# A prologue in a new order, one more softmax half summed on ScalarE, and slots 6 to 11 of a fused attention and MoE kernel rearranged

## The chip, the core and the metric

The kernel runs on one core of a Trainium2 chip. The metric is the device time of one execution in microseconds (us). TensorE (PE) multiplies, VectorE (DVE), ScalarE (ACT) and GpSimd (POOL) do the elementwise work, and SyncE (SP) issues most of the transfers from and to HBM. Each engine works through its own queue in the order in which the program issued its instructions; engines wait for each other by semaphores.

## The reference

Three stages, each fed by the one before it, in float32:

```python
# 1. chunked attention: q, k, v are (8 batches, 8 heads, 576, 64), in chunks of 64 rows
scores = scale * q_c @ k_c.T                      # 64x64 for each chunk
attn = exp(scores - max(scores)); attn /= sum(attn) + 1e-9
x = attn @ v_c                                    # -> (8, 576, 512)
# 2. gated feed-forward with a convolution over 3 neighbouring rows
h = relu(x @ w_in)                                # (8, 576, 1024)
gate = sigmoid(conv3(h))                          # each of the 1024 columns by itself
x = (h * gate) @ w_out                            # (8, 576, 512)
# 3. spatial gating
h = relu(x @ w_in2); u, v = h[..., :512], h[..., 512:]
v_s = w_spatial @ layernorm(v) + b_spatial
out = (u * v_s) @ w_out2
```

The four weight matrices come as float64 words, which the kernel turns into float32 itself.

## The kernel before

The 4608 rows of stages 1 and 2 are cut into ten tiles (eight of 512 rows, two of 256). Stage 2 of a tile has eight column blocks of 128, and **a slot is one tile and one column block**: slot s is tile s // 8 and block s % 8. Slots 0 to 7 are the first tile, 8 to 15 the second. A second phase (stage 3) follows, which the change does not touch.

To multiply float32 at the fast rate, each operand is split in a high and a low part (`xh`, `xl`; `w1h`, `w1l`; `gh`, `gl`; `w2h`, `w2l`), and a product is three terms: high by high, and the two mixed ones. The high part is a ScalarE cast, the low part a subtraction on VectorE (L83, `split_lo`) or, for some weights, on GpSimd. In a slot stand:

- **in(s)**, `moe_in`, L465: x times the block of w_in into the PSUM tile `h`, twelve matmuls of 512 columns. There are two such PSUM buffers.
- **h**, `moe_h`, L491: ScalarE's relu (`hh`, L498) and the middle tap of the convolution (`c`, L502), then two taps on VectorE (L517). From slot 8 on two edge elements at batch borders are mended on ScalarE (`m`, L513, and the "fix", L526).
- **g**, `moe_tanh` and `moe_g`, L523 and L530, for the slot before: ScalarE's tanh, VectorE's product (L532).
- **split**, `moe_split`, L535: `gh` on ScalarE, `gl` on VectorE.
- **out(s)**, `moe_out`, L552: the gated block times w_out, added up over a tile's eight blocks in four PSUM banks `acc`. The first five slots use plain float32 (`w2f`), all others three terms, twelve matmuls of 512 columns. After a tile's last block four ScalarE copies (`x`, L573) empty the banks.

The attention of one tile is two groups of 256 rows (group g; 0 and 1 belong to the first tile, 2 and 3 to the second, 4 and 5 to the third). The steps of a group are spread over the slots ahead of the tile that needs it. They are: scores `s` (L262); for each half j of the heads the softmax, which is the maximum and the subtraction on VectorE (L277, L283), the exp on ScalarE, and total, eps, reciprocal and norm on VectorE (L317 to L326); the transpose `tp` on TensorE (L362) and its copy `pt` on ScalarE (L368); then the product with v, `px` (L404), its cast `xh` on ScalarE (L439) and its low part `xl` on VectorE (L83). For a half named in `ACC` (L48) the exp is eight ScalarE activations of 64 columns, each of which also adds up its row sums (L301); VectorE then does neither the subtraction nor the total.

The order is written out by hand. `phase_a` first issues a prologue (L598 to L661): loads, scores and softmax of groups 0 and 1, the first weights. Between them `keep_warm` (L590) issues padding matmuls `pw` on TensorE: wide ones of 256 columns, or tiny ones of 16 columns where the second argument is 0. Slots 0 to 8 are issued by `start_slot`, which runs named steps in the order of a string: `ORDER` (L60) for slots 0 to 7 and `LAST_ORDER` (L61) for slot 8. From slot 9 (`START`, L63) the loop at L777 has a fixed order. `FIRST_SLOTS` (L56) says in which slots the scores and the product of a group stand: group 4 has its scores in slot 9 and its product in slot 11, group 5 in 13 and 16. The product stands at the end of its slot, or at its head ("front", L799) for groups from 5 on. Weights arrive piece by piece (`Pieces`, L118): load, `scale` on ScalarE (L94), `merge` on VectorE (L98, L102), then `high` and `low` or `part`.

Of the kernel before, what the change touches and what calls it, by code (L numbers as in the profile page):

```python
# [22 lines left out]
KF = FF // 128  # L23
# [24 lines left out]
ACC = ((0, 1), (2, 0), (2, 1), (3, 0), (3, 1))  # L48
RBUFS = 4
SPLIT = 5  # L50
NPAD = 6
# [4 lines left out]
FIRST_SLOTS = {1: ((1, 5), (5, 8)), 2: ((1, 5), (3, 8)), 3: ((0, 4), (4, 7))}  # L56
# [4 lines left out]
LAST_ORDER = "hh tp0 pv s g pt0 norm1 tp1 gs load merge exp0 norm0 x out in h pt1 exp1 split scale max"  # L61
NS = KF * NT
START = KF + 1  # L63
# [12 lines left out]
def attention_moe_kernel(ctx: ExitStack, tc: tile.TileContext, qT, kT, vL, vP, eye, w1, cw, w2, w3, wsp, wsr, bsp, w4, out):  # L76
# [104 lines left out]
    def phase_a(mid):  # L181
# [192 lines left out]
        def att_pv(g):  # L374
# [9 lines left out]
            if g < NP:  # L384
# [6 lines left out]
                elif g < PAIRED:  # L391
                    px = [ps_a.tile([128, 512], F32, tag=f"a{odd}", name="px") for odd in range(2)]
                else:
                    px = [ps_h.tile([128, 512], F32, tag="h", name="px") for _ in range(2)]
# [70 lines left out]
        def moe_in(s, parts=None):  # L465
# [7 lines left out]
            for p in parts or (slice(0, w),):  # L473
                n = 0
                for wt, x in terms if s > KF else (terms[0], terms[2], terms[1]):
# [15 lines left out]
        def moe_h(s, between=lambda: None):  # L491
# [6 lines left out]
            nc.scalar.activation(out=h[:, b:], in_=ph, func=AF.Relu)  # L498
            if i < NT - 1:
# [52 lines left out]
        def moe_out(s):  # L552
# [11 lines left out]
            for j, (w, x) in enumerate(terms):  # L564
                for m in range(KD):
# [60 lines left out]
        s1((1,))  # L626
        keep_warm(NPAD, 0)
        att_sm2((0, 0))
        att_sm1((1, 0))
        keep_warm(6)  # L630
        att_tp(0, 0)()
        att_exp(1, 0)
        att_sm1((1, 1))
        att_exp(1, 1)
        first.scale(2)
        att_sm2((0, 1))
        keep_warm(12)
        att_tp(0, 1)()
        att_sm2((1, 0))
        x0h, x0 = att_pv(0)  # L640
# [6 lines left out]
        keep_warm(8)  # L647
# [24 lines left out]
        def scores(s):  # L672
            if s in at:
# [4 lines left out]
                for j in range(2):  # L678
                    if s < START:
                        todo.setdefault((s, 1), []).append((g, j))  # L680
                        todo[s + 1 + j, 2 + j] = [(g, j)]
# [11 lines left out]
        def values(s):  # L693
# [5 lines left out]
            return (lambda: None,) * 2  # L699

        def start_slot(s):
# [27 lines left out]
            def half_tile():  # L729
# [3 lines left out]
                if s > SPLIT:  # L733
                    f, k, _ = first.wait.pop(SPLIT)
                    first.part(f, w2s["w2h"][:, k, :], w2s["w2l"][:, k, :], nc.vector)
                    moe_split(s - 1)

            def loads():
# [14 lines left out]
                "exp1": lambda: exps(3),  # L753
                "norm0": lambda: att_sm2(*todo.pop((s, 8), [])),
                "norm1": lambda: att_sm2(*todo.pop((s, 4), [])),
                "g": tanh_g,
                "gs": half_tile,
# [385 lines left out]
```

## Time and profile before

| | us |
|---|---|
| median of 3 runs | 898.66 (897.63 to 898.84) |
| the profiled execution | 899.47 |
| its span, first to last instruction | 897.7 |
| TensorE busy | 881.7 (98%) |
| VectorE busy | 565.6 (63%) |
| ScalarE busy | 485.2 (54%) |

TensorE is busy nearly throughout, so a microsecond of TensorE that is saved, or a wait of TensorE that goes, can shorten the run. Busy time alone doesn't tell whether a matmul runs at the full clock: a throttle grants TensorE one of two levels, 1.2 or 2.4 GHz, shown as the granted clock (0.5 or 1.0; the mean of a stretch lies between). The shares are means over the span: in its first half the other two engines are busy for 50 to 90% of most of the page's slices, and in the second half for much less.

All times below are counted from the start of the span. In rows of the timeline the first two numbers are the start of an instruction (or of a run of equal ones) and its length, and the bracket at the end tells how long the engine was idle before it and what ended that.

### The profile page before, as it was taken

The page shows a single profiled execution, that of the slowest core. Times are in us where ns is not written, and L with a number is a line of the kernel's source. Part 1 is how long each engine was busy: PE and PEld are TensorE (multiplying, and loading weights), DVE is VectorE, ACT ScalarE, POOL GpSimd, SP SyncE. Part 2 cuts the span into 40 slices and gives each one's busy share as a digit, 9 for nine tenths or more (in the row PEclk, how much of TensorE's full clock was granted, in tenths as well). Part 3 has the DMA queues.
Part 4 walks back from the last instruction along what each step waited for, and adds up shares of the span by engine and source line. Part 5 has one row for each costly group of instructions (what it writes and reads, how often), then busy time and mean ns, then how long its engine had stood idle before and what let it go on. Part 6 is the DMA issues. An engine that isn't in the chain of part 4 may idle for free.

```text
span 897.7 us, 17280 instructions
## 1 busy us (share of the span) xinstructions
PE 881.7 (98%) x6857; PEld 765.9 (85%) x6857; DVE 565.6 (63%) x1062; ACT 485.2 (54%) x1110; POOL 68.5 (8%) x197
## 2 busy tenths in 40 slices
PE   8999899999999999999999999999999999999998
PEld 7667688888878888778998989899898989989897
DVE  6996887878888888767675772716346171733422
ACT  5777768677676767677675633333334242332322
POOL 0000310111011111000000200100001000100000
PEclk9999899999999999999999999999999999999999
DMA  9922233434344534310334302040200302020001
GB/s 312 350 71 74 92 100 115 125 99 147 102 140 119 161 91 138 95 59 9 104 90 150 111 14 100 1 122 14 87 15 21 103 13 87 14 83 1 36 13 59
DMA packets 64593, 81.63 MB, mean 91 GB/s; under 512 B 7680, under 2 KB 51840, under 8 KB 64384
## 3 DMA queue, kind: packets, MB, share of 16 engines
q1 hardware_dynamic: 63280, 79.41, 28.2%
q8 instruction: 54, 0.88, 0.4%
q10 hardware_dynamic: 1232, 1.11, 0.4%
q14 instruction: 27, 0.22, 0.1%
HBM read 54.29 MB, written 18.87 MB: 82 GB/s over the span
## 4 chain that ended last, share of the span: by engine, by line
PE 77%; DVE 11%; ACT 8%; DMA 1%; issue 1%; SPq 1%; ACTq 0%; POOL 0%; DVEq 0%; POOLq 0%
PE acc L566 14%; PE pss L1017 13%; PE h L477 12%; PE psu L983 11%; PE psv L931 11%; PE pso L1036 11%; DVE c L517 4%; PE s L262 2%; ACT c L528 1%; PE x L423 1%; ACT c L502 1%; ACT hh L498 1%; DVE mx L277 1%; ACT c L526 1%; ACT e L306 1%
## 5 line engine op out<-in xcount | busy, mean ns | idle before, releaser
L517 DVE SCALAR_TENSOR_TENSOR c<-hh,nr,c 128x512 f32<-128x512 f32 (+3 forms) x160 | 112.0, 700 | 42.1 <-ACT c L502 39.0
L1019 DVE TENSOR_TENSOR gf<-pss,bb 128x288 f32<-128x288 f32 x64 | 29.0, 453 | 143.5 <-PE pss L1017 143.5
L477 PE MATMUL h<-xh,w1h 128*128 128x512 f32 (+1 forms) x324 | 81.2, 372 | 0.8 <-ACT w1h L155 0.8
L566 PE MATMUL acc<-gh,w2h 128*128 128x512 f32 (+2 forms) x300 | 77.9, 380 | 1.6 <-issue 1.3
L1021 ACT CAST gth<-gf 128x288 fp32r<-128x288 f32 x64 | 27.7, 433 | 95.4 <-DVE gf L1020 95.4
L477 PE MATMUL h<-xl,w1h 128*128 128x512 f32 (+1 forms) x324 | 78.8, 365 | 0.0
L477 PE MATMUL h<-xh,w1l 128*128 128x512 f32 (+1 forms) x324 | 78.7, 365 | 0.0
L1017 PE MATMUL pss<-wsh,vh 128*128 128x288 f32 x256 | 75.7, 296 | 0.0
L1017 PE MATMUL pss<-wsl,vh 128*128 128x288 f32 x256 | 75.4, 294 | 0.0
L1017 PE MATMUL pss<-wsh,vl 128*128 128x288 f32 x256 | 75.4, 294 | 0.0
L566 PE MATMUL acc<-gh,w2l 128*128 128x512 f32 (+2 forms) x300 | 74.3, 370 | 0.0
L566 PE MATMUL acc<-gl,w2h 128*128 128x512 f32 (+2 forms) x300 | 74.1, 369 | 0.0
L477 PEld LDWEIGHTS h<-xh,w1h 128*128 128x128 f32 x324 | 56.5, 188 | 12.3 <-ACT w1h L155 1.0
L477 PEld LDWEIGHTS h<-xl,w1h 128*128 128x128 f32 x324 | 56.9, 188 | 10.1
L477 PEld LDWEIGHTS h<-xh,w1l 128*128 128x128 f32 x324 | 56.9, 188 | 10.0
L566 PEld LDWEIGHTS acc<-gh,w2h 128*128 128x128 f32 x300 | 51.8, 190 | 12.2 <-ACT x L573 2.4
L532 DVE SCALAR_TENSOR_TENSOR c<-c,hh 128x512 f32<-128x512 f32 (+2 forms) x80 | 50.7, 634 | 18.0 <-ACT c L528 17.2
L566 PEld LDWEIGHTS acc<-gl,w2h 128*128 128x128 f32 x300 | 53.5, 190 | 9.7
L566 PEld LDWEIGHTS acc<-gh,w2l 128*128 128x128 f32 x300 | 53.5, 190 | 9.6
L526 ACT ACTIVATE c<-hh,m,nr 128x1 f32<-128x1 f32 x112 | 37.5, 385 | 42.5 <-DVE c L517 42.5
L987 ACT ACTIVATE u<-psu 128x288 f32<-128x288 f32 x64 | 26.3, 412 | 61.4 <-PE psu L983 61.4
L502 ACT ACTIVATE c<-hh,nr 128x512 f32<-128x512 f32 (+2 forms) x80 | 54.5, 682 | 7.2 <-POOL carry L500 0.4
(133 smaller groups left out, 1854.0 us busy)
## 6 DMA issues: line engine op xcount, KB each, us to landing
raw<-in_w_dram SPq DMA_DIRECT2D x18, 512.0 KB, 6.3
x2f<-x2d SPq DMA_DIRECT2D x32, 288.0 KB, 3.5
q<-in_qT_dram SPq DMA_DIRECT2D x16, 512.0 KB, 5.1
k<-in_kT_dram SPq DMA_DIRECT2D x16, 512.0 KB, 6.0
out_dram<-o SPq DMA_DIRECT2D x32, 256.0 KB, 2.1
pt<-t SPq DMA_DIRECT2D x160, 32.0 KB, 1.9
v<-in_vP_dram SPq DMA_DIRECT2D x8, 512.0 KB, 6.5
w_raw<-in_w_dram SPq DMA_DIRECT2D x8, 512.0 KB, 9.7
```

The lines of the kernel that those rows point to most:

```text
L477: nc.tensor.matmul(hs[s][:, p], wt[:, k, f * 128:(f + 1) * 128], x[:, k, b + p.start:b + p.stop], start=n == 0, stop=n == 11,)
L502: nc.scalar.activation(out=c, in_=h[:, o:o + n], func=AF.Copy, scale=cws[:, 1, f:f + 1])
L517: nc.vector.scalar_tensor_tensor(out=c[:, a:z], in0=h[:, o + a + step:o + z + step], scalar=cws[:, tap, f:f + 1], in1=c[:, a:z], op0=ALU.m ...
L526: nc.scalar.activation(out=dst, in_=src, func=AF.Identity, scale=w, bias=m)
L532: nc.vector.scalar_tensor_tensor(out=c, in0=c, scalar=1.0, in1=h, op0=ALU.add, op1=ALU.mult)
L566: nc.tensor.matmul(accs[m], w[:, f, m * 128:(m + 1) * 128], x, start=f == 0 and j == 0, stop=f == KF - 1 and j == len(terms) - 1,)
L931: nc.tensor.matmul(ps, x[:, k, sl], w[:, k, DV:], start=i == 0, stop=i == 11)
L983: nc.tensor.matmul(ps[:, :HB], w[:, k, d * 128:(d + 1) * 128], x[:, k, t], start=i == 0, stop=i == 11)
L1017: nc.tensor.matmul(o, a[:, ds], w, start=i == 0, stop=i == len(mm) - 1)
L1019: nc.vector.tensor_tensor(out=gf, in0=o, in1=bb[:, t], op=ALU.add)
L1021: nc.scalar.copy(out=gh[:, d, t], in_=gf)
L1036: nc.tensor.matmul(ps, x[:, k, sl], w[:, k, :], start=i == 0, stop=i == 11)
```

## The change

Four things change, all of them in the order of the program, apart from one softmax half.

1. Half (1, 0), the first half of group 1, joins `ACC`: its exps become eight activations with row sums on ScalarE, in place of a subtraction and a total on VectorE and one wide exp.
2. The prologue is reissued in another order with other padding: the softmax pieces, the copies `pt` of group 0, the scaling and merging of the second weight piece, and the terms of the second half of in(0), where xl now comes last.
3. Slots 6 to 9 have orders of their own (`ORDERS`), and slot 9 is now issued by `start_slot` (START is 10). In slot 6 the exps of group 3's second half stand behind the relu of that slot; in slot 7 the two transposes of group 3 stand behind in(7) and between the terms of out(5); in slot 8 group 3's product comes first, into the `h` buffers, and group 4's scores right behind it, and both halves of group 4's softmax are done in that slot; in slot 9 group 4's two transposes follow in(9).
4. Group 4's product stands at the head of slot 10, and group 5's scores in slot 11, behind in(11), in place of slot 13.

```diff
-ACC = ((0, 1), (2, 0), (2, 1), (3, 0), (3, 1))
+ACC = ((0, 1), (1, 0), (2, 0), (2, 1), (3, 0), (3, 1))
-NPAD = 6
+MPAD = 5
+NPAD = 13
-FIRST_SLOTS = {1: ((1, 5), (5, 8)), 2: ((1, 5), (3, 8)), 3: ((0, 4), (4, 7))}
+FIRST_SLOTS = {1: ((1, 5), (5, 8)), 2: ((0, 3), (2, 8)), 3: ((0, 4), (4, 7))}
-LAST_ORDER = "hh tp0 pv s g pt0 norm1 tp1 gs load merge exp0 norm0 x out in h pt1 exp1 split scale max"
+ORDERS = {
+    6: "hh in pv g exp1 load merge x norm1 exp0 norm0 out s tp0 gs h exp2 pt0 split scale tp1 pt1 max",
+    7: "hh in tp0 g pt0 norm1 load merge out1 cast split2 h1 split scale",
+    8: "hh pv s x g cast max split2 exp0 norm0 out in h",
+    9: "hh in tp0 tp1 pt0 pt1 g h out part",
+}
-START = KF + 1
+START = KF + 2
...
-                elif g < PAIRED:
+                elif g < PAIRED and g != P0 + 1:
...
-                for wt, x in terms if s > KF else (terms[0], terms[2], terms[1]):
+                for wt, x in terms if late or s > KF else (terms[0], terms[2], terms[1]):
...
             nc.scalar.activation(out=h[:, b:], in_=ph, func=AF.Relu)
+            behind()
...
             for j, (w, x) in enumerate(terms):
+                if j == 2:
+                    between()
...
+        att_sm2((0, 0))
+        pt00 = att_tp(0, 0)
+        att_sm1((1, 0))
+        att_exp(1, 0)
         keep_warm(NPAD, 0)
-        att_sm2((0, 0))
-        att_sm1((1, 0))
-        keep_warm(6)
-        att_tp(0, 0)()
-        att_exp(1, 0)
+        keep_warm(4)
+        att_sm2((0, 1))
         att_sm1((1, 1))
+        pt01 = att_tp(0, 1)
+        pt00()
+        pt01()
         att_exp(1, 1)
-        first.scale(2)
-        att_sm2((0, 1))
-        keep_warm(12)
-        att_tp(0, 1)()
+        first.scale()
         att_sm2((1, 0))
+        keep_warm(9)
...
         weave(first.merge())
-        keep_warm(8)
+        keep_warm(3)
         att_tp(1, 1)()
         first.high()
         x0()
         first.low()
+        first.scale()
+        keep_warm(3)
         x1h, x1 = att_pv(1)
         moe_in(0, (slice(0, 256),))
         x1h()
+        weave(first.merge())
         x1()
-        moe_in(0, (slice(256, 512),))
+        first.high()
+        moe_in(0, (slice(256, 512),), True)
+        keep_warm(MPAD, 0)
         weave(merge_steps(cw_words))
-        weave(first.merge())
-        first.high()
         first.low()
         first.scale(2)
...
+                    if s == KF:
+                        for k in (1, 2, 8):
+                            todo.setdefault((s, k), []).append((g, j))
+                        todo[s + 1, 5 + j] = [(g, j)]
+                    elif s < START:
                         todo.setdefault((s, 1), []).append((g, j))
-                        todo[s + 1 + j, 2 + j] = [(g, j)]
+                        todo[s + 1 + j * (g == P0), 2 + j + 7 * j * (g > P0)] = [(g, j)]
...
-            front = pv_at.get(s, 0) >= PAIRED
+            front = pv_at.get(s, 0) >= PAIRED or s == START
             if front:
                 xs = values(s)
                 xs[0]()
+            if s == START + 1:
+                moe_in(s)
             scores(s)
```

The prologue on TensorE, before and now, from the scores of groups 0 and 1 (`s`) to the first product (`h`); `pw` are padding matmuls, `tp` the transposes, `px` the products with v. Before:

```order
L262 MATMUL s<-k,q 64x64 x64
L596 MATMUL pw<-warm 16x16 x6
L594 MATMUL pw<-warm 64x256 x6
L362 MATMUL tp<-idt,e 128x128 x4
L594 MATMUL pw<-warm 64x256 x12
L362 MATMUL tp<-idt,e 128x128 x4
L404 MATMUL px<-pt,v 64x64 x32
L362 MATMUL tp<-idt,e 128x128 x4
L594 MATMUL pw<-warm 64x256 x8
L362 MATMUL tp<-idt,e 128x128 x4
L404 MATMUL px<-pt,v 64x64 x32
L477 MATMUL h<-xh,w1h 128x256 x4
```

Now, on the same engine and from the same place:

```order
L268 MATMUL s<-k,q 64x64 x64
L368 MATMUL tp<-idt,e 128x128 x4
L605 MATMUL pw<-warm 16x16 x13
L603 MATMUL pw<-warm 64x256 x4
L368 MATMUL tp<-idt,e 128x128 x4
L603 MATMUL pw<-warm 64x256 x9
L410 MATMUL px<-pt,v 64x64 x32
L368 MATMUL tp<-idt,e 128x128 x4
L603 MATMUL pw<-warm 64x256 x3
L368 MATMUL tp<-idt,e 128x128 x4
L603 MATMUL pw<-warm 64x256 x3
L410 MATMUL px<-pt,v 64x64 x32
```

The first transpose moved ahead of the padding, and the wide padding matmuls between the scores and the first product went from 26 to 19.

ScalarE in slots 6 and 7, from the weight cast of slot 6 (`w2h`) on; `e,sm<-s,mx` are the eight exps of group 3's second half, `c<-c` the tanh, `pt` the copies of group 3's transposes. Before:

```order
L150 CAST w2h<-w2f 128x512
L541 CAST gh<-c 128x512
L498 ACTIVATE hh<-h 128x512
L502 ACTIVATE c<-hh,nr 128x512
L528 ACTIVATE c<-c 128x512
L301 ACTIVATE e,sm<-s,mx 128x64 x8
L150 CAST w2h<-w2f 128x512
L541 CAST gh<-c 128x512
L498 ACTIVATE hh<-h 128x512
L502 ACTIVATE c<-hh,nr 128x512
L368 COPY pt<-tp 128x512 x2
```

Now:

```order
L759 CAST w2h<-w2f 128x512
L548 CAST gh<-c 128x512
L504 ACTIVATE hh<-h 128x512
L509 ACTIVATE c<-hh,nr 128x512
L307 ACTIVATE e,sm<-s,mx 128x64 x8
L535 ACTIVATE c<-c 128x512
L374 COPY pt<-tp 128x512
L759 CAST w2h<-w2f 128x512
L548 CAST gh<-c 128x512
L504 ACTIVATE hh<-h 128x512
L374 COPY pt<-tp 128x512
L509 ACTIVATE c<-hh,nr 128x512
```

The eight exps moved ahead of the tanh, and the two copies stand apart and ahead of the convolution's middle tap.

VectorE in slots 9 to 11, with the softmax of group 4: `mx` the maxima, `e<-s,mx` the subtractions, `sm` totals and eps, `rs` reciprocals, `e<-e,rs` norms, `c<-hh,nr,c` the convolution's taps, `c<-c,hh` the gate's product. Before, from the taps of slot 8:

```order
L517 SCALAR_TENSOR_TENSOR c<-hh,nr,c 128x512 x2
L277 TENSOR_REDUCE mx<-s 128x8
L283 TENSOR_TENSOR e<-s,mx 128x512
L532 SCALAR_TENSOR_TENSOR c<-c,hh 128x512
L317 TENSOR_REDUCE sm<-e 128x8
L320 TENSOR_SCALAR sm<-sm 128x8
L323 RECIPROCAL rs<-sm 128x8
L326 TENSOR_TENSOR e<-e,rs 128x512
L517 SCALAR_TENSOR_TENSOR c<-hh,nr,c 128x512 x2
L83 TENSOR_TENSOR gl<-c,gh 128x512
```

Now, from the product of slot 7's gate:

```order
L539 SCALAR_TENSOR_TENSOR c<-c,hh 128x512
L283 TENSOR_REDUCE mx<-s 128x8 x2
L289 TENSOR_TENSOR e<-s,mx 128x512 x2
L89 TENSOR_TENSOR w2l<-w2f,w2h 128x512
L89 TENSOR_TENSOR gl<-c,gh 128x512
L323 TENSOR_REDUCE sm<-e 128x8 x2
L326 TENSOR_SCALAR sm<-sm 128x8 x2
L329 RECIPROCAL rs<-sm 128x8 x2
L332 TENSOR_TENSOR e<-e,rs 128x512 x2
L524 SCALAR_TENSOR_TENSOR c<-hh,nr,c 128x512 x2
```

Both halves are done together, ahead of the taps of slot 8, where before they stood one by one behind the taps of slots 8 and 9.

## Rows read from the trace of the kernel before

**Rows 1.** Busy time by stretch: engines, then granted clock, DMA share, GB/s.

```profile
25.00:92.00 67.00, 65.13 (x548) 46.15 (x548) 56.48 (x103) 52.22 (x144) 5.83 (x14) 1.00 0.48 164
94.00:101.00 7.00, 6.16 (x20) 4.57 (x20) 5.90 (x7) 5.33 (x14) 2.63 (x3) 0.51 0.00 0
```

**Rows 2.** Timeline of TensorE, slots 7 to 14.

```profile
66.61 1.07 PE L566 MATMUL acc<-gh,w2h 128*128 128x512 f32 x4
...
70.57 0.63 PE L362 MATMUL tp<-idt,e 128*128 128x128 f32 x4 [0.64 <-DVE e L326]
72.06 0.33 PE L404 MATMUL px<-pt,v 64*64 64x64 f32 x2 [0.86 <-ACT pt L368]
...
94.84 1.08 PE L362 MATMUL tp<-idt,e 128*128 128x128 f32 x4 [2.74 <-DVE e L326]
...
100.96 1.16 PE L404 MATMUL px<-pt,v 64*64 64x64 f32 x64
102.06 1.20 PE L477 MATMUL h<-xh,w1h 128*128 128x512 f32 x4
...
107.73 1.16 PE L262 MATMUL s<-k,q 64*64 64x64 f32 x64
108.82 1.19 PE L477 MATMUL h<-xh,w1h 128*128 128x512 f32 x4
...
114.39 1.07 PE L477 MATMUL h<-xh,w1h 128*128 128x512 f32 x4
...
117.12 0.60 PE L362 MATMUL tp<-idt,e 128*128 128x128 f32 x4
117.47 1.17 PE L566 MATMUL acc<-gh,w2h 128*128 128x512 f32 x4
```

**Rows 3.** Timeline of ScalarE, slots 7 to 12.

```profile
66.80 0.30 ACT L301 ACTIVATE e<-s,mx 128x64 f32<-128x64 f32 x1
...
69.11 0.65 ACT L150 CAST w2h<-w2f 128x512 fp32r<-128x512 f32 x1
...
86.36 2.03 ACT L573 ACTIVATE x<-acc 128x512 f32<-128x512 f32 x4
...
90.00 0.63 ACT L528 ACTIVATE c<-c 128x512 f32<-128x512 f32 x1
...
92.71 0.58 ACT L498 ACTIVATE hh<-h 128x512 f32<-128x512 f32 x1
...
94.39 0.56 ACT L368 COPY pt<-tp 128x512 f32<-128x512 f32 x1
...
102.18 1.07 ACT L439 CAST xh<-px 128x512 fp32r<-128x512 f32 x2 [2.46 <-PE px L404]
```

**Rows 4.** Timeline of VectorE, slots 10 and 11.

```profile
89.45 1.37 DVE L83 TENSOR_TENSOR gl<-c,gh 128x512 fp32r<-128x512 f32 x1 [1.57 <-ACT gh L541]
...
94.61 1.53 DVE L517 SCALAR_TENSOR_TENSOR c<-hh,nr,c 128x512 f32<-128x512 f32 x2
```

**Rows 5.** Timeline of TensorE, prologue.

```profile
16.68 0.93 PE L404 MATMUL px<-pt,v 64*64 64x64 f32 x48 [0.42 <-ACT pt L368]
...
25.20 1.19 PE L477 MATMUL h<-xh,w1h 128*128 128x512 f32 x4 [0.81 <-ACT w1h L155]
```

**Rows 6.** Timeline of ScalarE, prologue.

```profile
9.29 0.31 ACT L301 ACTIVATE e<-s,mx 128x64 f32<-128x64 f32 x1 [0.99 <-DVE mx L280]
...
24.53 0.62 ACT L155 CAST w1h<-nr 128x512 fp32r<-128x512 f32 x1 [2.24 <-DVE nr L102]
```

**Rows 7.** Timeline of VectorE, prologue.

```profile
16.78 0.68 DVE L317 TENSOR_REDUCE sm<-e 128x8 f32<-128x512 f32 x1
...
18.55 0.42 DVE L98 TENSOR_SCALAR raw<-raw 128x512 uint32<-128x512 uint32 x1
...
21.84 1.29 DVE L83 TENSOR_TENSOR xl<-px,xh 128x512 fp32r<-128x512 f32 x2 [0.27 <-ACT xh L439]
...
23.35 0.42 DVE L98 TENSOR_SCALAR raw<-raw 128x512 uint32<-128x512 uint32 x1
```

More of the change, by code (lines that the diff above doesn't have):

```diff
@@ L463, in outputs, with moe_in @@
             return 1, width(i), TOKEN[i] - 1
-        def moe_in(s, parts=None):
+        def moe_in(s, parts=None, late=False):
             i, f = divmod(s, KF)
@@ L489, in moe_hh, with moe_h @@
             hhs[s] = h
-        def moe_h(s, between=lambda: None):
+        def moe_h(s, between=lambda: None, behind=lambda: None):
             i, f = divmod(s, KF)
@@ L550, in store, with moe_out @@
                 nc.sync.dma_start(out=dst, in_=src)
-        def moe_out(s):
+        def moe_out(s, between=lambda: None):
             i, f = divmod(s, KF)
@@ L678, in scores @@
                 for j in range(2):
-                    if s < START:
+                    if s == KF:
[3 more added lines that the diff above has]
+                    elif s < START:
                         todo.setdefault((s, 1), []).append((g, j))
-                        todo[s + 1 + j, 2 + j] = [(g, j)]
+                        todo[s + 1 + j * (g == P0), 2 + j + 7 * j * (g > P0)] = [(g, j)]
                         todo[s + 1, 8] = [(g, 0)]
@@ L699, in values, with spare_part @@
             return (lambda: None,) * 2
+        def spare_part():
+            if first.wait:
+                f, k, _ = first.wait.pop(0)
+                first.part(f, w2s["w2h"][:, k, :], w2s["w2l"][:, k, :])
         def start_slot(s):
@@ L727, in tanh_g, with cast @@
                     moe_g(s - 1)
-            def half_tile():
+            def cast():
                 if s == SPLIT + 1:
@@ L734, in half_tile @@
                     f, k, _ = first.wait.pop(SPLIT)
-                    first.part(f, w2s["w2h"][:, k, :], w2s["w2l"][:, k, :], nc.vector)
+                    w = w2s["w2h"][:, k, :], w2s["w2l"][:, k, :]
+                    nc.scalar.copy(out=w[0], in_=f)
+                    pend["w"] = lambda: split_lo(nc.vector, w[1], f, w[0])
+            def half_tile():
+                if s > SPLIT:
+                    pend.pop("w")()
                     moe_split(s - 1)
@@ L753, in start_slot @@
                 "exp1": lambda: exps(3),
+                "exp2": lambda: exps(10),
                 "norm0": lambda: att_sm2(*todo.pop((s, 8), [])),
@@ L756, in start_slot @@
                 "g": tanh_g,
-                "gs": half_tile,
+                "cast": cast,
+                "split2": half_tile,
+                "gs": lambda: (cast(), half_tile()),
+                "part": spare_part,
                 "load": loads,
@@ L762, in start_slot @@
                 "out": lambda: moe_out(s - LAG0) if s >= LAG0 else None,
+                "out1": lambda: moe_out(s - LAG0, lambda: transposes(6)),
+                "h1": lambda: moe_h(s, behind=lambda: call(6)),
                 "h": lambda: moe_h(s),
@@ L767, in start_slot @@
             }
-            for k in (ORDER if s < KF else LAST_ORDER).split():
+            for k in ORDERS.get(s, ORDER).split():
                 steps[k]()
@@ L807, in phase_a @@
                 xs[1]()
-            if START + 1 <= s < NS + 2:
+            if START <= s < NS + 2:
                 moe_split(s - 2)
@@ L821, in phase_a @@
             if s < NS:
-                moe_in(s)
+                if s != START + 1:
+                    moe_in(s)
                 if tp:
@@ L834, in phase_a @@
             if first.wait:
-                f, k, _ = first.wait.pop(0)
-                first.part(f, w2s["w2h"][:, k, :], w2s["w2l"][:, k, :])
+                spare_part()
             elif s > 2 * KF and s % 4 == 0:
```

## The prediction

> **What bounds the kernel now.** I read the busy shares by stretch first: TensorE is busy 65.13 of the 67 us from 25 to 92 at a granted clock of 1.00, with VectorE at 56.48 beside it; from 94 to 101 the granted clock is 0.51, which is the lower of its two levels (1.2 of 2.4 GHz) [rows 1]. So the time is TensorE's, and a gain must come from places where it waits or runs at half clock. Then I read TensorE in order of time. In slots 7 and 8 it waits 0.64 us for the second half of group g=3's softmax and 0.86 us for the copy of its transpose; in slot 11 it waits 2.74 us for a softmax half of g=4, and the work behind that wait is slow [rows 2]. Behind slot 13 no wait of that kind follows. Last I read ScalarE and VectorE ahead of those waits, and the first 25 us, where TensorE waits twice for ScalarE (0.42 and 0.81 us) and otherwise runs padding matmuls [rows 3 to 7].
>
> **Slots 7 to 12: what is lost there now.** I take the stretch from the end of slot 7's first product (66.61) to the start of slot 13's (108.82): 42.21 us [rows 2]. It holds ten blocks of twelve wide matmuls (products out(5) to out(9) and in(8) to in(12)), two px, two s, four tp. In(13) with out(10) runs from 108.82 to 114.39, 5.57 us, so one block is 2.785; px is 1.10 (100.96 to 102.06), s 1.09 (107.73 to 108.82), tp 0.35 (117.12 to 117.47) [rows 2]. 27.85 + 2.20 + 2.18 + 1.40 = 33.63 us. Lost: 42.21 - 33.63 = 8.58 us. Of that 0.64 + 0.86 + 2.74 = 4.24 are the waits; tp and out(8) from 94.84 to 100.96 take 6.12 where full clock gives 0.35 + 2.785, so half clock costs 2.98; the other 1.36 I put down to the array draining and refilling around the waits and to the narrow matmuls.
>
> The change adds no work for TensorE here; it moves where the waits fall. The same stretch afterwards also holds the first tp of g=5 (0.35), which is only moved. I walk the three places where it may wait, in the times of the run before:
>
> *Slot 7, second tp of g=3.* Its eight exps stand now at 66.80, behind the tanh of slot 7, and end at 69.11: 2.31 us [rows 3]. They move to slot 6, in front of that tanh, to about 64.55, and end at 66.85. The tanh (0.55), VectorE's gate product (0.6) and the short tail eps, reciprocal, norm (from the end of the exps to the tp that waited it is 69.11 to 70.57 today, 1.46, with the issue of all steps [rows 2, 3]; I take 1.3 since part of it was ScalarE's signal) bring the tp to 69.3. TensorE is there after tp and two thirds of out(5): 66.61 + 0.35 + 1.86 = 68.8. Wait 0.5. The last third of out(5), 0.93, then covers the copy that px waited 0.86 for. Bounds: 0 to the 1.50 of today.
>
> *Slot 9, both tp of g=4.* s(g=4) goes to slot 8 and its two halves are done together. TensorE: 69.3 + 0.35 + 0.93 + px 1.10 + s 1.09 = 72.8, then out(6), in(8), in(9): 81.1. VectorE has from the end of px (71.7) ScalarE's cast of it (about 1.0 [rows 3]), then 13 wide operations and four short ones: xl 2, gate 1, max 2, subtract 2, w2l, gl, total 2, norm 2. The xl pair takes 1.29 for two [rows 7], so 13 x 0.62 + 0.4 = 8.5, and 72.7 + 8.5 = 81.2; the first half is ready 0.6 sooner. Wait about 0, bounds 0 to the 2.74 of today. Here the covers are four blocks of TensorE instead of two.
>
> *Slot 12, first tp of g=5.* TensorE: 81.1 + two tp 0.7 + out(7) 2.8 = 84.6, px 1.1, in(10), in(11), s, out(8), in(12): 97.9. ScalarE: the conv taps of slot 8 stand behind the norms (81.2 + 1.45), then fix and tanh (1.25, to its end from 90.00 less the fix before it), relu, conv and edge terms of slot 9 (92.71 to 94.39, 1.68) bring it to 85.7, where the four copies of out(7)'s sums come (86.36 to 90.00 with two casts and the fixes, tanh to 90.6: 4.2 us), the cast of g=4's px put into that queue (1.0), and relu and conv of slot 10 (1.3): 92.2 [rows 3]. The taps take 1.45 (the pair's 1.53 with its tail [rows 4]): VectorE reaches gl(9) at 93.65. From that gl to the tp it is 5.39 us today (89.45 to 94.84 [rows 2, 4]): 99.0. Wait 1.1. That is the new wait: g=5's softmax comes two slots sooner, behind everything that slot 10 queues. Behind it only out(9) is queued on TensorE. Bounds 0 to 2.74.
>
> The row of that gl shows 1.37 us, about twice what one of the xl pair takes (1.29 for two) [rows 4, 7]; the tail of 5.39 holds this slow gl. The Trainium skill (SBUF — State Buffer, "SBUF: two separate sides") says that VectorE and GpSimd share a port pair under an exclusive lock and that the loser waits for the whole instruction of the other; this row agrees with it (1.37), since a GpSimd split is issued just ahead of that gl. The rule speaks against the change where slots 9 and 10 put such splits ahead of gl(8) and gl(9): a collision at gl(8) too would make slot 12's wait 1.8 by it, and none at either would make it 0.4.
>
> Sum: the waits 0.5 + 0 + 1.1, and 0.5 for draining at two waits instead of four, against 8.58: gain 6.5 us. If no wait is left, 8.6; if slot 12's wait equals today's 2.74 at full clock, 4.8.
>
> **Prologue.** Now the second transposed copy of group 0 stands behind three other ScalarE pieces, and px's second part starts at 16.68, having waited for it [rows 5]. After: the exps of (0,1) start at 9.29 [rows 6] and the eight of (1,0) follow on them, so these end near 9.29 + 2 x 2.31 = 13.9, say 14.2 as their maximum must come first; two copies at 0.55 end at 15.3, 1.4 us sooner. That half costs ScalarE 1.8 us more than one wide exp, and saves VectorE a subtract and a total (1.3). The last half's exp follows at 15.8, so its total, now at 16.78, starts at 15.85, and the merge of the first weights, now at 18.55, at 17.6 [rows 7]. From there to xl of group 1 it is 3.29 now (18.55 to 21.84) with 0.27 of waiting in it; add the merge of the second weights, moved ahead of it (23.35 to the cast at 24.53: 1.18 [rows 6, 7]): 17.6 + 3.0 + 1.2 = 21.8, and xl ends at 23.1. The second half of the first product now takes xl last, so it ends at 23.7; five tiny pads 0.1; slot 1 starts at 23.8 instead of 25.20 [rows 5]. Its weights' cast, which TensorE waits for today, is done at 22.4. Gain 1.4. Bounds: 0 if another link (a weight's landing, v for px) holds it at 25.2, and 2.1 if the chain runs without any of my allowances. Of the padding, 26 wide matmuls between scores and first product become 19, with 18 tiny ones for 6; they fill waits, and cost nothing while the clock stays. Slots 1 to 6 keep their order but for g=3's exps; VectorE, busy 56.48 of 67 us there [rows 1], gets its slot 1 work about 2 us sooner, so 1.4 passes through to 66.61. All weights are issued to the DMA queue in the order of before.
>
> **Sum.** 6.5 + 1.4 = 7.9. The profiled execution took 899.47, so 891.6; the median of the three runs lies 0.81 below it: 890.8. TensorE works without a long wait from there on, so nothing behind slot 13 should give it back.
>
> **Rivals.** (B) *One wait keeps its length and the clock falls once more.* If VectorE reaches slot 12's softmax 1.6 us later than worked, the wait is 2.74 again and half clock costs 2.98 again: 890.8 + 1.6 + 3.0 = 895.4. For it: ScalarE's queue in slots 9 and 10 is a chain of estimates without slack. Against: the waits of 0.64 and 0.86 in slots 7 and 8 did not lower the clock [rows 1, 2]. (C) *The prologue gives nothing*, since a link I can't see holds slot 1 at 25.2: 892.2; with the clock falling over the thinner padding, 895.2. For it: the DMA queues are full there; against: both visible waits are on ScalarE. (D) *The other side: the backlog of slots 8 to 10 outlasts TensorE's cover at all three tp of g=4 and g=5 (slots 9, 12, 13)*: two halves at once on VectorE, ScalarE's eight exps in slot 6, the extra cast in slot 10. Each wait of 2.74 brings half clock at 2.98: 5.7 + 4.6 + 5.7 = 16.0, so 906.8. It decides once VectorE is 2.7 us later at slot 9 than worked. Against: VectorE still had 1.57 us of idle time in before's slot 10, just ahead of the gl [rows 4]. (E) *It doesn't do what it says*: the waits are only renamed, as the same VectorE and ScalarE work stands between the same ends, and the time is 898 to 899. Against: a third of the loss (2.98 of 8.58) is a clock that falls after one wait, and splitting that wait is enough to keep it.
>
> **How the numbers follow.** Forecast 0.68, with 889.0 to 892.6 as its own range; B 0.13, C 0.11, D 0.04, E 0.04. The range that holds the time 8 times in 10 is 888.6 (no wait left) to 894.5 (C and the milder part of B). A measurement of this kernel can tell about 0.2%, 1.8 us, from no change: faster by more than that 0.92, within it 0.04, slower 0.04.
>
> **What would show it.** Right: no stretch under full clock between 25 us and the last tile; slot 1's product at about 23.8; tp in slot 7 waiting about 0.5, in slot 9 hardly, in slot 12 about 1; slot 13's product about 7.9 us earlier than 108.82. Wrong: a granted clock near 0.5 anywhere between 65 and 105 us, a wait of over 2 us at g=5's tp, or slot 1's product at 25.

## The result, and the profile after

| | before | changed |
|---|---|---|
| median, same chip | 898.14 us (897.56 to 898.84, 4 runs) | 892.14 us (891.74 to 892.20, 4 runs) |
| ratio | | 0.9915, interval 0.9896 to 0.9933 |
| profiled execution | 899.47 | 892.2 |
| its span | 897.7 | 890.4 |

The changed kernel is faster by 6.0 us of the medians and by 7.3 us of the two profiled executions; forecast were a median of 890.8 us and a gain of 7.9 us. A second group of runs, on another chip, gave 891.73 us and 0.9918 (0.9898 to 0.9938).

The busy shares of the same two stretches as in [rows 1]:

```profile
25.00:92.00 67.00, 67.00 (x681) 48.13 (x680) 57.36 (x108) 54.62 (x150) 4.22 (x15) 1.00 0.51 172
94.00:101.00 7.00, 5.96 (x29) 4.71 (x28) 6.73 (x11) 3.64 (x10) 2.55 (x4) 1.00 0.36 126
```

TensorE is busy in all 67 us of the first stretch (65.13 before), and the granted clock of the second is 1.00 where it was 0.51: the half clock of slot 11 is gone. TensorE's timeline shows what the waits of [rows 2] became:

```profile
65.85 0.60 PE L368 MATMUL tp<-idt,e 128*128 128x128 f32 x4
...
68.14 0.60 PE L368 MATMUL tp<-idt,e 128*128 128x128 f32 x4
...
69.60 1.16 PE L410 MATMUL px<-pt,v 64*64 64x64 f32 x64
...
79.96 1.03 PE L368 MATMUL tp<-idt,e 128*128 128x128 f32 x8
...
98.32 0.63 PE L368 MATMUL tp<-idt,e 128*128 128x128 f32 x4 [1.03 <-DVE e L332]
...
101.55 1.07 PE L483 MATMUL h<-xh,w1h 128*128 128x512 f32 x4
...
105.17 0.63 PE L368 MATMUL tp<-idt,e 128*128 128x128 f32 x4 [0.73 <-DVE e L332]
...
121.38 1.20 PE L575 MATMUL acc<-gh,w2h 128*128 128x512 f32 x4
```

Neither transpose of g=3 in slot 7 waits, nor px behind them, nor the two of g=4 in slot 9 (79.96). g=5's first transpose waits 1.03 us in slot 12 and its second 0.73 us in slot 13. From the end of in(7), 65.85, to in(13), 101.55, it is 35.70 us, where it was 42.21: 6.51 less, and 6.5 was forecast. The stretch holds one transpose (0.35) more than before. Up to the first matmul of out behind slot 16's scores (121.38), where both programs have done the same work, the gain is 6.23: 55.53 us from the end of in(7), where it was 61.76 (66.61 to 128.37).

The end of the prologue on TensorE, which answers to [rows 5]:

```profile
22.66 0.74 PE L483 MATMUL h<-xl,w1h 128*128 128x256 f32 x4 [0.36 <-DVE xl L89]
23.24 0.17 PE L605 MATMUL pw<-warm 128*16 128x16 f32 x1
24.34 0.26 PE L605 MATMUL pw<-warm 128*16 128x16 f32 x4 [0.93 <-issue]
24.47 1.17 PE L483 MATMUL h<-xh,w1h 128*128 128x512 f32 x4
```

The first product ends at 23.24, where 23.7 was forecast; the second part of the scores, which wait for their loads, also began sooner in this execution (6.46 against 7.10). But in the tiny padding TensorE stands for 0.93 us with nothing to wait for ("issue"), and slot 1's product starts at 24.47: 0.73 us sooner than 25.20, not 1.4.

The two profiled executions differ by 0.76 up to the end of in(7), 6.51 in the stretch, and then by smaller things that the change did not aim at, and that happen to cancel: less 0.28 for slot 13's wait (two transposes of g=5 stood behind in(13) before, one does now), less 0.36 between 263 and 288 us, plus 1.47 around 370 us, where the kernel before had an issue stall of 1.33, and less 0.83 between 408 and 470 us. The sum is 7.27.

### The profile page after: what moved, and what is told of

The parts are those of the page before. It is cut to its first block, busy times and chain, and to the rows that moved or that the text cites. A ratio compares the mean times of both kernels' runs of the same rounds, so it can differ in the third digit from the quotient of the medians.

```text
span 890.4 us, 17308 instructions
## 1 busy us (share of the span) xinstructions
PE 878.6 (99%) x6862; PEld 764.0 (86%) x6862; DVE 563.1 (63%) x1061; ACT 487.5 (55%) x1125; POOL 66.9 (8%) x197
## 4 chain that ended last, share of the span: by engine, by line
PE 81%; DVE 10%; ACT 6%; DMA 1%; issue 1%; SPq 1%; ACTq 0%; DVEq 0%
PE acc L575 16%; PE h L483 14%; PE pss L1054 13%; PE psu L1020 11%; PE psv L968 11%; PE pso L1073 11%; DVE c L524 3%; PE s L268 2%; PE x L429 1%; ACT c L533 1%; DVE e L332 1%; DVE sm L323 1%; ACT c L535 1%; DVE e L289 1%; DVE gl L89 1%; ACT hh L504 1%
```

## The experiments

Medians are compared with the kernel before in the same group of runs. It had 899.06 us in the first group (the first four experiments), 899.94 in the second (the next four) and 899.02 in the third.

| experiment | median us (range) | ratio to before, interval |
|---|---|---|
| old prologue | 894.81 (892.03 to 896.19) | 0.9949, 0.9930 to 0.9967 |
| new prologue alone | 896.25 (895.21 to 898.46) | 0.9969, 0.9957 to 0.9981 |
| pads early | 892.56 (891.94 to 892.68) | 0.9925, 0.9906 to 0.9944 |
| fewer instructions | 894.01 (890.70 to 896.24) | 0.9943, 0.9922 to 0.9964 |
| g=5's scores late | 890.02 (889.73 to 890.53) | 0.9885, 0.9869 to 0.9901 |
| splits on VectorE | 890.09 (889.96 to 890.98) | 0.9889, 0.9875 to 0.9903 |
| slots 6, 7 undone | 892.81 (892.51 to 893.05) | 0.9917, 0.9903 to 0.9931 |
| one long wait | 895.07 (893.17 to 896.02) | 0.9940, 0.9926 to 0.9954 |
| changed kernel again | 891.73 (891.06 to 893.10) | 0.9918, 0.9898 to 0.9938 |
| both edits | 889.89 (889.76 to 890.33) | 0.9897, 0.9880 to 0.9915 |
| both, fewer instructions | 890.28 (888.25 to 895.21) | 0.9908, 0.9883 to 0.9934 |

### The orders without the prologue

```diff
-ACC = ((0, 1), (1, 0), (2, 0), (2, 1), (3, 0), (3, 1))
+ACC = ((0, 1), (2, 0), (2, 1), (3, 0), (3, 1))
...
-        att_sm2((0, 0))
-        pt00 = att_tp(0, 0)
...
```

What is left out is the diff of the prologue, reversed.

> The changed kernel with the prologue of before (softmax half (1,0) back on VectorE, its padding too); slots 6 to 11 stay as changed. The theory: the orders of slots 6 to 11 carry 6.5 us by themselves and the new prologue gave only what slot 1's start shows, 0.73 us, plus the slot-7 wait that its lead took away; so 892.1 + 0.7 to 1.2 = 892.8 to 893.3, slot 1's product near 25.2, slot 7's second tp waiting 0.5 or less, no stretch under full clock. A rival, that the prologue's 1.4 us was earned in full through ScalarE and VectorE: 893.5 or more. A second rival, that slots 6 to 9 depend on the lead and the clock falls without it: 895 or more.

Slot 1's product starts at 25.41, slot 7's second transpose waits 0.35 us, those in slots 12 and 13 as in the changed kernel, and the clock stays at 1.00:

```profile
69.65 0.63 PE L368 MATMUL tp<-idt,e 128*128 128x128 f32 x4 [0.35 <-DVE e L332]
```

In(13) starts at 103.06, 1.51 us later than in the changed kernel's trace: 0.94 from slot 1's start and the rest from slot 7. The median is further off, 894.81 against 892.8 to 893.3 expected, and would fit the first rival (893.5 or more); but this trace holds an issue stall of 1.35 us at 365 us that the changed kernel's does not, and 1.51 is what it shows of the prologue. The second rival, that the orders need the lead, falls: the waits of 2.74 and half clock do not come back.

### The prologue without the orders

The kernel before, with the prologue, its padding and `ACC` as changed.

```diff
-ACC = ((0, 1), (2, 0), (2, 1), (3, 0), (3, 1))
+ACC = ((0, 1), (1, 0), (2, 0), (2, 1), (3, 0), (3, 1))
...
-                for wt, x in terms if s > KF else (terms[0], terms[2], terms[1]):
+                for wt, x in terms if late or s > KF else (terms[0], terms[2], terms[1]):
```

> The kernel before with the new prologue alone. The theory: slot 1's product starts at 24.5 instead of 25.2 and TensorE passes that on to slot 7, but the waits of 0.64, 0.86 and 2.74 us and the half clock behind the last stay, since no order there is changed: 0.7 us less than before, at most 1.4 (897.4 to 896.7). The rival, that the prologue's lead is lost in the waits of slots 7, 8 and 11, which then grow: no change, 898.1. A stall at the start of slot 1's product (issue, about 0.9 us) should be there as in the changed kernel, since the count of TensorE's instructions ahead of it is the same.

It gains 2.8 us (1.7 to 3.9), more than either expectation. The profiled execution is the slowest of the twelve (898.46). Slot 1's product starts at 25.32 only, since the second part of the scores came 1.6 us later than in the changed kernel's trace (8.01 against 6.46), and in(0) 1.9 us later. Yet the second transpose of g=3 waits 0.17 instead of 0.64, the wait in slot 11 is shorter, and the clock behind it stays:

```profile
94.17 0.63 PE L363 MATMUL tp<-idt,e 128*128 128x128 f32 x4 [2.46 <-DVE e L327]
```

```profile
94.00:101.00 7.00, 5.54 (x84) 4.46 (x85) 5.34 (x8) 5.38 (x13) 2.66 (x3) 1.00 0.01 2
```

2.46 us instead of 2.74, granted clock 1.00 instead of 0.51; part of it is lost again to px, which waits 1.29 us (to 99.10). The stretch from in(7) to in(13) is 40.25 us instead of 42.21. No issue stall stood ahead of slot 1 here, so that part of the expectation was wrong.

### How long a wait costs the clock

```diff
-                nc.vector.reduce_max(out=mx[:, :nu, 0], in_=ps, axis=AX.X)
+                for _ in range(4 if (g, j) == (5, 0) else 1):
+                    nc.vector.reduce_max(out=mx[:, :nu, 0], in_=ps, axis=AX.X)
```

> The changed kernel with the maximum of group 5's first softmax half taken four times over (three more VectorE instructions at 0.71 us), so that slot 12's wait of 1.03 us becomes about 3.1 us in one piece, longer than the 2.74 us wait behind which the clock of the kernel before fell. The theory of the prediction (a wait of this length lets the granted clock fall to half for some 6 us): 2.1 for the wait and 3.0 for half clock, 897.2, with a stretch at granted clock near 0.5 behind 98. The rival (the fall in the kernel before came from the waits of slots 7, 8 and 11 together, or from what TensorE did between them): 2.1 alone, 894.2, at full clock.

```profile
100.65 1.09 PE L369 MATMUL tp<-idt,e 128*128 128x128 f32 x4 [3.21 <-DVE e L333]
101.39 2.06 PE L576 MATMUL acc<-gh,w2h 128*128 128x512 f32 x4
...
106.59 1.08 PE L484 MATMUL h<-xh,w1h 128*128 128x512 f32 x4
```

```profile
100.00:106.00 6.00, 5.35 (x15) 4.42 (x16) 5.83 (x8) 3.73 (x9) 2.02 (x2) 0.50 0.00 0
```

One wait of 3.21 us, with none in slots 7, 8 and 11 ahead of it, lets the clock fall to its lower level (0.50): tp and out take 5.94 us (100.65 to 106.59) instead of 3.14, so 2.8 us, near the 2.98 of the kernel before. The rival falls: one long wait is enough. Wait and clock cost what was expected (2.18 more of wait and 2.8 of clock, 5.0 together), but the medians rose by 2.9 to 3.3 us only: slot 13's wait of 0.73 went, since TensorE came there later, and the changed kernel's traces lose 0.8 to the slow pace of matmuls told of under hardware, which this one does not.

### The kernel before once more

No edit.

> The kernel before once more, unedited, for a second trace. Theory: its wait in slot 11 is 2.5 to 2.8 us again; the half clock behind it depends on a tenth or two of that wait (it stood behind 2.74 and 3.21 us and not behind 2.46), so it may be there or not; the issue stall of 1.33 near 370 us stands at the same instruction. Rival: the half clock is there in every execution, with about 3 us.

One run, 898.0 us. The wait is the same, the half clock behind it shorter:

```profile
95.15 1.09 PE L362 MATMUL tp<-idt,e 128*128 128x128 f32 x4 [2.73 <-DVE e L326]
95.89 2.06 PE L566 MATMUL acc<-gh,w2h 128*128 128x512 f32 x4
...
99.84 1.38 PE L404 MATMUL px<-pt,v 64*64 64x64 f32 x64
```

From tp to px it is 4.69 us instead of 6.12, so half clock costs 1.55 here and not 2.98, and the stretch to in(13) 41.0 instead of 42.2. Both theory and rival were half right: the fall was there in both executions, its price was not the same. The stall of 1.33 us at 370 us is absent, so the expectation that it stands at the same instruction again was wrong.

### Slots 6 and 7 undone

```diff
-    6: "hh in pv g exp1 load merge x norm1 exp0 norm0 out s tp0 gs h exp2 pt0 split scale tp1 pt1 max",
-    7: "hh in tp0 g pt0 norm1 load merge out1 cast split2 h1 split scale",
-                        todo[s + 1 + j * (g == P0), 2 + j + 7 * j * (g > P0)] = [(g, j)]
+                        todo[s + 1 + j, 2 + j] = [(g, j)]
```

> The changed kernel with slots 6 and 7 in the order of before (the exps of group 3's second half behind the tanh of slot 7, its two transposes together behind slot 7). The theory: the waits of 0.64 and 0.86 us that stood in slots 7 and 8 of the kernel before come back in part, and what follows keeps its cover and full clock: 1.0 to 1.7 us more, 893.1 to 893.8. A rival, that group 4's softmax in slot 8 is then late too, since ScalarE is held by those exps: a wait at slot 9's transposes of 1 us or more, and with it 895 or more. A second rival, that those orders gave nothing: 892.1.

```profile
70.83 1.42 PE L408 MATMUL px<-pt,v 64*64 64x64 f32 x64 [0.87 <-ACT pt L372]
```

The wait for the copy of g=3's transposes is back at 0.87 us (0.86 before), the stretch from in(7) to in(13) is 37.16 instead of 35.70 (1.46 more), and nothing behind it changes. The wait of 0.64 does not come back. The median is 0.7 to 1.1 us above the changed kernel's two, in other groups, where 1.0 to 1.7 were expected; but the changed kernel's traces lose 0.8 to the slow pace of matmuls told of under hardware, which this one does not. So the finding rests on the stretch.

### What the early scores of group 5 cost

```diff
-FIRST_SLOTS = {1: ((1, 5), (5, 8)), 2: ((0, 3), (2, 8)), 3: ((0, 4), (4, 7))}
+FIRST_SLOTS = {1: ((1, 5), (5, 8)), 2: ((0, 5), (2, 8)), 3: ((0, 4), (4, 7))}
```

> The changed kernel with the scores of group 5 back in slot 13, as before the change; all else stays. The theory: the waits of 1.03 us in slot 12 and 0.73 us in slot 13 are the price of group 5's early scores alone, and go; behind slot 13 its softmax has cover enough: 1.5 to 1.8 us less, 890.3 to 890.6. A rival, that the work queued in slot 10 on ScalarE and VectorE stays late whatever stands behind it and the wait only appears in slot 14 or 15: 891.5 to 892.1, with waits of 0.7 or more at group 5's transposes.

Both waits of g=5's transposes are gone, the stretch is 33.88 us (the working had 33.63 for its bare work), and one wait appears in slot 16:

```profile
118.41 0.93 PE L410 MATMUL px<-pt,v 64*64 64x64 f32 x48 [1.03 <-ACT pt L374]
```

Up to the same matmul behind slot 16's scores it is 54.69 us from the end of in(7), 0.84 less than in the changed kernel. The median, 890.02 us, is 1.7 to 2.1 below the changed kernel's two, in other groups; part of that is again the slow pace. So moving group 5's scores to slot 11 was a loss inside the change, and the gain does not need it.

### Whose port the late softmax waited for

```diff
-                first.part(f, w2s["w2h"][:, k, :], w2s["w2l"][:, k, :])
+                first.part(f, w2s["w2h"][:, k, :], w2s["w2l"][:, k, :], nc.vector)
```

> The changed kernel with the weight splits of the spare pieces in slots 9 to 13 (w2l, five of 512 columns) on VectorE in place of GpSimd. The theory: gl(9) took 1.78 us and the taps behind it 2.44 us because a GpSimd split ran beside them; alone they take 0.68 and 1.5, while VectorE gains a split of 0.65 in each slot. Slot 12's wait 1.03 falls by 1.1 less 0.65, to about 0.5, and slot 13's of 0.73 falls by the same order: 891.2 to 891.7. The rival (those instructions are long for another reason): they stay at 1.8 and 2.4, the waits grow by 0.65 each: 893.0 to 893.4.

GpSimd and VectorE in the changed kernel, then VectorE with the splits on it:

```profile
91.99 1.76 POOL L89 TENSOR_TENSOR w2l<-w2f,w2h 128x512 fp32r<-128x512 f32 x1 [1.47 <-ACT w2h L156]
```

```profile
91.06 1.54 DVE L524 SCALAR_TENSOR_TENSOR c<-hh,nr,c 128x512 f32<-128x512 f32 x2 [0.61 <-ACT c L509]
92.51 1.78 DVE L89 TENSOR_TENSOR gl<-c,gh 128x512 fp32r<-128x512 f32 x1
...
98.09 2.44 DVE L524 SCALAR_TENSOR_TENSOR c<-hh,nr,c 128x512 f32<-128x512 f32 x2
```

```profile
92.09 0.68 DVE L89 TENSOR_TENSOR w2l<-w2f,w2h 128x512 fp32r<-128x512 f32 x1
92.69 0.69 DVE L89 TENSOR_TENSOR gl<-c,gh 128x512 fp32r<-128x512 f32 x1
...
97.19 1.53 DVE L524 SCALAR_TENSOR_TENSOR c<-hh,nr,c 128x512 f32<-128x512 f32 x2
```

gl goes from 1.78 to 0.69 and the taps from 2.44 to 1.53, with GpSimd's splits gone from beside them (the second one, 1.43 us, ran from 98.55). gl and the added split together are shorter than gl alone was. The waits fall to 0.57 and 0.46, as worked out. The time fell by more than these rows give (0.48 in the stretch and 0.27 in slot 13 against 1.6 to 2.0 us of the medians); 0.8 of the rest is the slow pace of matmuls told of under hardware, which the two traces of the changed kernel have and this one has not. The Trainium skill (SBUF — State Buffer, "SBUF: two separate sides") has VectorE and GpSimd under one exclusive port lock in which the loser waits for the other's whole instruction; 1.78 for 0.69 beside a split of 1.76 agrees with it.

### Both edits

The two one-line edits above together.

> The changed kernel with both edits that helped: group 5's scores in slot 13 and the spare weight splits of slots 9 to 13 on VectorE. Theory: both take away the same two waits (1.03 and 0.73 us), so together they give little more than either alone: 2.0 to 2.5 us less than the changed kernel, 889.6 to 890.2. Rival: the gains add up (each took 2 us), 888.1; a second rival: VectorE, with the splits on it, is late at another transpose and it is slower than either, 891.

```profile
117.00 0.93 PE L410 MATMUL px<-pt,v 64*64 64x64 f32 x48 [0.23 <-ACT pt L374]
```

889.89 us, 1.84 less than the changed kernel's 891.73 beside it, and 0.1 to 0.2 less than either edit alone. Those ran in another group, though, and without the slow pace told of under hardware, which this trace has; so the traces are the better measure, from the end of in(7) to the same matmul behind slot 16's scores:

| kernel | from, to | us |
|---|---|---|
| changed, two traces | 65.85, 121.38 and 65.20, 120.74 | 55.53 and 55.54 |
| g=5's scores late | 65.51, 120.20 | 54.69 |
| splits on VectorE | 65.42, 120.21 | 54.79 |
| both edits | 64.92, 118.80 | 53.88 |

The gains are 0.84 and 0.74 alone and 1.66 together: they add up, as the first rival had it, though each is less than the 2 us it put on them. The two edits do not take away the same waits only. With g=5's scores late and the splits on GpSimd, the wait in slot 16 stood behind slow taps:

```profile
106.39 2.44 DVE L524 SCALAR_TENSOR_TENSOR c<-hh,nr,c 128x512 f32<-128x512 f32 x2
```

A split of 1.44 us ran beside them from 106.85. Without it they take 1.53 (from 105.30), and the wait of 1.03 shrinks to 0.23. The kernel with both edits beats the kernel before and the changed one, and its runs differ little.

### The stall at the head of slot 1

```diff
-MPAD = 5
-NPAD = 13
+MPAD = 0
+NPAD = 18
```

> The changed kernel with the five tiny padding matmuls that stand ahead of slot 1's product moved up to the 13 behind the first transpose: the same number of TensorE instructions ahead of that product, none of them padding right ahead of it. The theory (TensorE runs out of fetched instructions after a fixed count of them, while the transfers of the weights fill the queues): a stall of about 0.9 us marked issue stays there, slot 1's product starts at 24.3 to 24.5, time as the changed kernel's, 892.1 within 0.3. The rival (the tiny pads themselves hold the sequencer): the stall goes, slot 1's product starts near 23.3 to 23.5, and the time falls by up to 0.9, to 891.2.

```profile
24.68 0.74 PE L483 MATMUL h<-xl,w1h 128*128 128x256 f32 x4 [2.04 <-DVE raw L104]
25.26 1.09 PE L483 MATMUL h<-xh,w1h 128*128 128x512 f32 x4
```

The stall moved with the instruction count: five matmuls more stand ahead, and it falls on the last third of in(0). The row puts it down to VectorE, but xl was done there at 22.96, 1.72 us before the matmul started; the releaser named had long been done. Slot 1's product starts at 25.26, and the median is 892.56 beside the changed kernel's 892.14 and 891.73. The padding right ahead of that product is not the cause.

```diff
-MPAD = 5
-NPAD = 13
+MPAD = 0
+NPAD = 0
-        keep_warm(NPAD, 0)
-        keep_warm(4)
+        keep_warm(7)
```

> The changed kernel without any tiny padding matmul (18 fewer) and with 7 wide ones in place of 4 behind the first transpose: 15 fewer TensorE instructions ahead of slot 1's product, so that the count at which the stall stood falls inside that product and not ahead of it. The theory (fetch by count): the stall moves by 15 instructions, into slot 1's product, with the same 0.9 us or less, and what goes ahead of it (the start of slot 1's product) is at 23.3 to 23.5; the time falls by 0 to 0.9 (891.2 to 892.1) depending on how far the fetch then lags. The rival (pads): the stall is gone altogether and the time falls by 0.9 less what slot 7 waits again (0.5): 891.2 to 891.7.

No stall is seen ahead of slot 1 or in its product, where one was expected. But in this execution the second part of the scores came 1.5 us later than in the changed kernel's trace, in(0) started 2.0 us later, and slot 1's product started at 25.25 for that reason, so it tells nothing of the gain. A longer stall came later, and the clock fell with it:

```profile
243.24 0.48 PE L268 MATMUL s<-k,q 64*64 64x64 f32 x3 [2.83 <-issue]
243.65 2.07 PE L575 MATMUL acc<-gh,w2h 128*128 128x512 f32 x4
```

So the median, 894.01, lies above the 891.2 to 892.1 expected. Its edit and both helpful ones together:

> As the run with both edits, and without the 18 tiny padding matmuls (three more wide ones), so that the count of TensorE instructions at which the issue stalls stood falls behind the start of slot 1's product. Theory: slot 1's product starts right behind the one before, 0.6 us after its last third begins, near 23.3 where the scores come as early as in the changed kernel; 0.5 to 0.9 us less than with both edits alone, unless a later stall at the same kind of count appears, as the 2.83 us near 240 us did: then 2 to 4 us more. Rival: the prologue's end is set by data, and slot 1's product starts at 24 or later with TensorE waiting for VectorE or ScalarE.

Slot 1's product starts right behind in(0), at 23.83; a stall of 2.56 us stands at 239.91 again, and the granted clock behind it stays at 1.00 this time. The fastest single run of all, 888.25 us, and one of 895.21 are of this kernel; its median gains nothing.

### The changed kernel once more

No edit.

> The changed kernel once more, unedited, as the yardstick of this group and for a second trace. Its first trace had 0.93 us of issue at the head of slot 1's product and, between 430 and 454 us, products of 256 columns that came every 0.47 us instead of 0.45, which is 0.8 us in all that the other kernels did not lose. Theory: the issue stall depends on how early the prologue gets there (slot 1's product starts near 24.0 to 24.6 in any case), and the 0.8 is of this one execution: 891 to 892.2. Rival: both are fixed by the program and stand here again with the same size, 892.1.

```profile
23.70 0.28 PE L605 MATMUL pw<-warm 128*16 128x16 f32 x5
23.84 1.17 PE L483 MATMUL h<-xh,w1h 128*128 128x512 f32 x4
...
97.67 0.63 PE L368 MATMUL tp<-idt,e 128*128 128x128 f32 x4 [1.03 <-DVE e L332]
104.51 0.63 PE L368 MATMUL tp<-idt,e 128*128 128x128 f32 x4 [0.73 <-DVE e L332]
```

The stall of 0.93 is absent and slot 1's product starts at 23.84. The scores' second part began at 7.21 here, close to the 7.10 of the kernel before. The waits 1.03 and 0.73, and the stretch of 35.70 us, are the same to the hundredth: these belong to the program, the stall to the execution. The slow pace between 430 and 454 us stands here again, so there the rival was right.

## Why the prediction was right

- *The place.* Right: the gain is in the stretch between in(7) and in(13), 6.51 of 7.27 us. That it meets the 6.5 worked out so closely is luck in part. With the transpose moved into it (0.35) the stretch has 33.98 us of bare work, so 1.72 are lost in it where 2.1 were forecast: 0 for 0.5 in slot 7, 1.03 for 1.1 in slot 12, and 0.69 for 0.5 of draining. Up to slot 16, with slot 13's wait in it, the gain is 6.23.
- *Half clock, 2.98 us.* Right in its cause and not in its constancy. One long wait brings it (2.73, 2.74 and 3.21 us; not 2.46), and so did an issue stall of 2.83 us, while one of 2.56 did not. But the same wait of the same kernel cost 2.98 in one execution and 1.55 in the other. With the second trace of the kernel before, the stretch's gain is 5.3 (41.01 to 35.70).
- *Slot 7's second transpose, 0.5.* Measured 0. The new prologue gave ScalarE a longer lead than TensorE: against the run with the old prologue the eight exps start 1.77 us sooner (62.98, 64.75), and in(7) ends 1.00 sooner. Without the new prologue the wait is 0.35.
- *Slot 9, 0.* Right.
- *Slot 12's first transpose, 1.1.* 1.03. One gl beside a GpSimd split was slow, 1.78 us, and gl of slot 8 was not (0.68): of the three cases weighed there, the middle one.
- *What was missed.* The second transpose of g=5 waits 0.73 in slot 13, since the taps ahead of it, 2.44 us, stood beside another split. The sum named no wait there. It held since 0.5 for slot 7 was not spent, and this wait falls behind the stretch.
- *The prologue, 1.4.* 1.36 in the second trace of the changed kernel, whose scores came about as in the trace before. 0.73 in the first, with a stall of TensorE's own supply that no row of before had shown at that place: a term that the sum did not have. Rival C (nothing) falls by either. Undoing the prologue cost 1.5 us up to in(13) by the traces.
- *From the profiled execution to the median, 0.81.* The forecast took the median 0.81 below the profiled execution, as in the kernel before. There the profiled execution held the stall of 1.33 at 370 us, which its second trace has not; in the changed kernel the two lie 0.06 apart (892.2, 892.14). With 7.27 for 7.9 this makes the 1.3 by which the median missed 890.8.
- *Rivals B and D* did not happen, but B's mechanism is real: the long wait of the experiment brought a half clock of 2.8 us. *Rival E* falls: no wait of before stands under a new name with its old length.
- Left open: the gain of each part by medians, 4.3 (3.0 to 6.3, orders) and 2.8 us (prologue), leaves the prologue twice what slot 1's start shows. Part is the shorter wait in slot 11 and the clock it saves, 1.96 us of the stretch against the first trace of before and 0.76 against the second; how often the old prologue's executions hold an issue stall is not known from two traces. No run undoes the move of group 4's softmax by itself: its part, the wait of 2.74 and the clock behind it, is what the other runs leave of the stretch's gain.

## What to carry to other kernels

Price a long wait of TensorE by what the clock does behind it: waits of about 1 us (1.03, 0.73, 0.86) left the clock at its upper level here, one of 2.7 cost up to twice its length, and one of 2.46 cost its length alone. So splitting a long wait, or shortening it by a few tenths, can be worth more than the time taken off it. When a step is moved earlier, look at what the queues ahead of it hold, and at which engine works beside them: here the early scores of group 5 brought 1.76 us of waits, and two one-line edits gave back 1.66 us. And before a difference of one or two microseconds is put down to an edit, take a second trace of both kernels, and compare a stretch that holds the same work rather than medians of different groups.

## What the runs showed of the hardware

*TensorE can run out of instructions.* Sixteen stalls of 0.16 to 2.83 us were seen in the fourteen traces, all but one marked "issue". Counted over all of TensorE's records in the trace (weight loads, matmuls and its sequencer's own), each comes when 449, 705, 4801, 5313 or 7105 of them have gone by, which is 193 more than a multiple of 256. The page of the changed kernel shows a queue that carries instructions, 54 packets and 0.88 MB, so some 16 KB each:

```profile
q8 instruction: 54, 0.88, 0.4%
```

Each trace has 54 such counts as well. Taken in order, the first packet with the second count and so on, TensorE went on in all sixteen stalls 1.3 to 1.8 us after the packet of that count had landed; at the counts without a stall it had landed 1.2 us or more before. In the changed kernel's first trace that packet landed at 22.89, and TensorE stood until 24.34 (count 705); in the second it landed at 20.56, and TensorE came to the same count at 23.70 and did not stand. So it is the delivery of instructions that TensorE waits for. What makes a packet late is not shown: the transfer queues were full ahead of slot 1 (DMA share 1.08 from 20 to 25 us), but not ahead of the stall of 2.83 us (0.46 from 236 to 243). The Trainium skill (Runtime: NRT & Kernel Launch, "Instruction fetch mechanics") has the fetch by blocks of 256 instructions and the cost of crossing into the next one mostly hidden. Both agree here, with sixteen stalls at some 750 crossings; but a crossing that is not hidden cost up to 2.83 us.

*Two paces of the same matmul.* Between 430 and 454 us four matmuls of 256 columns start every 0.47 us in the changed kernel's trace and every 0.45 in the one with the splits on VectorE, at full clock in both:

```profile
437.54 0.63 PE L483 MATMUL h<-xh,w1h 128*128 128x256 f32 x4
438.01 0.64 PE L483 MATMUL h<-xh,w1l 128*128 128x256 f32 x4
```

```profile
435.00 0.62 PE L575 MATMUL acc<-gh,w2l 128*128 128x256 f32 x4
435.45 0.62 PE L575 MATMUL acc<-gl,w2h 128*128 128x256 f32 x4
```

It is 0.8 us in all and was not explained. The slow pace stands in the first trace of the changed kernel and in all four traces of the third group, that of the kernel before among them; it stands in none of the eight traces of the first two groups, nor in the first of the kernel before. So it hides 0.8 us when medians of different groups are compared.
